# Moving one output copy, one chunk of v and one fill unit inside the step of a recurrent-memory transformer kernel

## The chip, the cores and the metric

The kernel runs on one core of one Trainium2 chip. The core has a matrix engine (TensorE, PE in the profile, with its weight loads shown apart as PEld), a vector engine (VectorE, DVE), a scalar engine (ScalarE, ACT), a general engine (GpSimd, POOL) and a queue engine (SyncE, SP) that issues most of the transfers. Each engine works through its own instructions in the order in which they were written; semaphores tie the engines together. The metric is the device time of one execution in microseconds (us), as the median of several runs.

## The reference

The input x has 2048 tokens of width 640. The first half of the computation is an attention with 32 heads of width 128 that goes through the tokens in 64 segments of 32, one after the other, and carries a memory of 8 rows from each segment to the next:

```python
for s in range(n_seg):
    xs = x[:, s * seg_len:(s + 1) * seg_len, :].copy()     # the layer-normed tokens
    h = jnp.concatenate([mem, xs], axis=1)                 # 8 memory rows and 32 tokens
    q = jnp.einsum('btd,dhe->bhte', h, Wq)
    k = jnp.einsum('btd,dhe->bhte', h, Wk)
    v = jnp.einsum('btd,dhe->bhte', h, Wv)
    scores = jnp.einsum('bhqe,bhke->bhqk', q, k) * scale
    scores = jnp.where(mask[None, None], scores, -1000000000.0)
    p = _softmax(scores, axis=-1)
    o = jnp.einsum('bhqk,bhke->bhqe', p, v)
    o = jnp.einsum('bhte,hed->btd', o, Wo)
    mem = o[:, :M, :].copy()
    outs.append(o[:, M:, :])
```

The memory rows of one segment's output are an input of the next segment, so the 64 segments are a chain. The second half adds the result to x, applies a second layer norm and a feed-forward layer (640 to 1728 and back, squared ReLU), and adds again. Everything is held in bf16, with sums in f32.

## The kernel before

The kernel has a start, 64 steps (one for each segment, function `step(b, sp)`, where segment s = 4 b + sp, so a block b of 128 tokens has the steps sp = 0 to 3), and the feed-forward part at the end. The change touches only the body of a step. There is no scheduler: the order in which the instructions are written is the order in which each engine runs them.

**What a step projects.** The 40 rows of a segment are split. 32 of them (8 memory rows and the first 24 tokens) are the "main" rows: `hT4s[b][:, c, sp, :]` holds them transposed, in five chunks c of 128 features. The last 8 tokens of each segment, the "tail" rows, don't depend on the memory. They are projected for four segments at once, ahead of time.

The projections go through `proj` (line 203): a chunk is four matmuls of 128x512 on the four column groups of TensorE. A half projection, five chunks, goes into one bank of the pool `mm`, which has three banks; ScalarE copies it out as a row (`evac_row`, lines 219 and 221; line 410 for the second half of k), and VectorE turns the row into qT or kT (`flip`, line 224; line 413). A step begins with half 0 of q, half 0 of k, half 1 of q and half 1 of k. Then come both halves of v, with the scores between their chunks. The copies of v's halves are on ScalarE, lines 508 (half 0) and 529 (half 1).

**Memory queries.** They come in two groups, n = 0 (even) and n = 1 (odd). For each group: `scores` (line 423), `soft1` (maximum on VectorE, line 429; exponential on ScalarE, line 432), `soft2` (lines 438 to 445, all on VectorE; the last one, pTm, is the transposed probabilities), `values` (lines 454 and 459 on TensorE, into the tile po) and `values_out` (n = 0 on VectorE, line 210; n = 1 on ScalarE, line 212), which puts them into oT. v's half 0 is an input of the even values.

**Token queries.** Their scores (line 499) go into the tile sk. Their softmax is lines 533 to 536 on VectorE, 551 on ScalarE, 553 and 557 on VectorE and 559 and 562 on POOL. The values of the step before are made one step late, in `token_values` (lines 359 and 364), and copied into oT by `token_out` (line 368, ScalarE): one half at the end of the step, the other at the start of the next.

**Output projection.** `wo_rounds` (line 235) runs 16 rounds of four matmuls of 128x320 into the tile pw: rounds 0 to 5, then token and odd memory values, then rounds 6 and 7, a fill unit, and rounds 8 to 15. pw holds two partial sums in its two lower and two upper groups of partitions, 32 rows each.

**From pw two things are made.** `mem_to_hT` (lines 252 to 255) makes the memory rows of the next step: VectorE transposes pw (two of line 252, tile otr), ScalarE copies the upper half (two of line 253, tile otc), VectorE adds (two of line 255) into hT. The next step's first matmul needs these. `wo_out` makes the whole output: ScalarE copies the upper half of pw to SBUF (line 242, tile otmp), VectorE adds it to the lower half (line 243, tile o, one of a ring of five), and `store_main` (line 346) issues two transfers on SP that store the 24 main token rows. otmp lives in the same buffer (tag "tk") as otr, and pw in the same bank (pool `chn`) as the next step's memory scores.

**Fill units.** The tail rows' projections (`tail_units`: v in sp = 0, q in sp = 1, k in sp = 2) and the output projection of four steps' tails (`wo_tail_units`, sp = 3) are cut into units, a chunk each or one to two wo rounds, and queued in the list `fill`. For the blocks 1 to 14 ten units are queued in the steps sp = 1 (q), 2 (k) and 3 (wo); in sp = 0 there are ten units of v in the blocks 4, 6, 8, 10 and 12, five in the blocks 5, 7, 9, 11, 13 and 14, and none in the others. `run(fill, 1)` runs one unit between rounds 7 and 8 and `run(fill, 100)` the rest at the end of the step, where they give TensorE work while the memory rows are made. The fifth unit of a half ends with that half's copy to a row on ScalarE; its flip is put into the list `late`, which the next step works off at several places.

**Other lists.** `win` holds the PE transposes of a normalised block or of tail rows: five transposes and their copies on ScalarE (line 189 for a block's rows, in the steps sp = 1; line 183, two copies, for tail rows, in two steps sp = 2). `mid` holds some normalisations. `owed` holds work of this step that the next one does: the second `token_out`, the turned token probabilities (lines 576 to 581) and `tokens_kept` (line 372).

The end of a step in the order before: `mem_to_hT`, lines 557 to 562, `wo_out` and `store_main`, `token_out` half 0, the transposes in `win` and their copies, the copies of tail q and k into qT and kT on POOL (`tails_in`, lines 328 and 330), `mid`, `fill`.

Of the kernel before, what the change touches and what calls it, by code (L numbers as in the profile page):

```python
# [16 lines left out]
def kernel(  # L17
# [25 lines left out]
    DC = D // 128  # L43
# [31 lines left out]
    wv = wts.tile([128, DC * HE], BF16)  # L75
# [117 lines left out]
    def proj(w, by, lhs, n, ps, c0, c1):  # L193

        if by == "columns":
            wr = w[:].rearrange("p (c g j n k e) -> p c n k g j e", c=DC, g=G, n=2, j=4, k=4)
        elif by == "half":
            wr = w[:].rearrange("p (c k j n e) -> p c n k j e", c=DC, k=G, n=2, j=4)
        else:
            wr = w[:].rearrange("p (c k n f) -> p c n k f", c=DC, k=G, n=2)  # L200
        for c in range(c0, c1):
            for k in range(4):
                nc.tensor.matmul(ps[32 * k:32 * k + 32, :], lhsT=lhs(c), rhs=wr[:, c, n, k], start=(c == 0), stop=(c == DC - 1))  # L203

    def mmtile():
        return mm.tile([128, 512], F32, tag="mm", name="ps")
# [31 lines left out]
    def wo_out(pw):  # L238
        o = o_ring[0]
        o_ring.append(o_ring.pop(0))  # L240
        tmp = s1.tile([128, DH], F32, tag="tk", name="otmp")
        nc.scalar.copy(out=tmp[0:64], in_=pw[64:128, 0:DH])
        nc.vector.tensor_tensor(out=o[:], in0=pw[0:64, 0:DH], in1=tmp[0:64], op=ALU.add)
        return o
# [12 lines left out]
    fill, late, mid, win, owed = [], [], [], [], [[], [], []]  # L257

    def run(q, n):
        while n > 0 and q:  # L260
            q.pop(0)()
            n -= 1
# [81 lines left out]
    def store_main(o, s):  # L344
        for ch in range(2):
            nc.sync.dma_start(out=o_all[s * SEG:s * SEG + HD, ch * DH:(ch + 1) * DH],
                              in_=o[32 * ch + M:32 * ch + 32, :])
# [37 lines left out]
    def step(b, sp, v=None):  # L385
        s = b * 4 + sp
        last = s == NS - 1
        hT4 = hT4s[b]
        lhs = lambda c: hT4[:, c, sp, :]
# [46 lines left out]
        def soft2(n):  # L436
            rm = s2.tile([128, 1], F32, tag="rm", name="rm")
            nc.vector.reciprocal(out=rm[:], in_=zms[n][:])
            pm = s2.tile([128, 2 * SEG], BF16, tag="pmem", name="pmem")
            nc.vector.tensor_scalar(out=pm[:, 0:SEG], in0=ems[n][:, 0:SEG], scalar1=rm[:, 0:1], scalar2=None, op0=ALU.mult)  # L440
            nc.vector.scalar_tensor_tensor(out=pm[:, SEG:2 * SEG].rearrange("p (j k) -> p j k", k=TL),
                                           in0=ems[n][:, SEG:NK].unsqueeze(1).to_broadcast([128, 4, TL]),
                                           scalar=rm[:, 0:1], in1=same[:], op0=ALU.mult, op1=ALU.mult)
            pT = s2.tile([128, 2 * SEG], BF16, tag="pTm", name="pTm")
            nc.vector.transpose(out=pT[:], in_=pm[:])
            return pT
# [64 lines left out]
        if not ready:  # L511
            ps1 = mmtile()
# [7 lines left out]
            run(fill, DC)  # L520
        po = pop.tile([128, G, 512], F32, tag="po", name="po")
        if not ready:
            proj(wv, "half", lhs, 1, ps1, 2, 3)
        if not last:
            values(0, pT0, po)
            values_out(0, po)
        if not ready:
            proj(wv, "half", lhs, 1, ps1, 3, DC)
            nc.scalar.copy(out=v[:, 512:1024], in_=ps1[:])  # L529
        if not last:  # L530
            pT1 = soft2(1)
        tk = s1.tile([128, HG, NK], F32, tag="tk", name="tk")
# [5 lines left out]
        pw = chn.tile([128, 512], F32, tag="ch", name="pw")  # L538
# [15 lines left out]
        if not last:  # L554
# [6 lines left out]
        pk = s1.tile([128, HG, 32], BF16, tag="pk", name="pk")  # L561
        nc.gpsimd.tensor_tensor(out=pk[:], in0=ek[:, :, 0:SEG], in1=rk[:].unsqueeze(2).to_broadcast([128, HG, SEG]),
                                op=ALU.mult)
        o = wo_out(pw)
        if s > 1:
            store_main(o, s - 2)
        if s:
            token_out(0, po)
            owed[0].append(lambda: token_out(1, po))
# [17 lines left out]
            tails_in((s + 1) // 4, (s + 1) % 4)  # L587
        run(mid, 2)
        run(fill, 100)
        if last:  # L590
            for q in owed:
                run(q, 100)
# [157 lines left out]
    for b in range(NB):  # L750
        for sp in range(4):
# [47 lines left out]
            if 2 <= e <= NK4 + 1:  # L799
                late.append(lambda e=e: prep_stats0(e - 2))  # L800
                mid.append(lambda e=e: prep_norm0(e - 2))
            step(b, sp, v0 if b + sp == 0 else None)

    def end_output(s):
# [112 lines left out]
```

## Time and profile before

| | |
|---|---|
| median of three runs | 1025.73 us (1023.66 to 1028.19) |
| the profiled execution's own time | 1020.01 us |
| its span | 1018.2 us |
| granted TensorE clock, mean | 0.998 |
| PE busy | 956.1 us (94%) |
| DVE busy | 697.4 us (68%) |
| ACT busy | 561.6 us (55%) |
| POOL busy | 261.6 us (26%) |

The profile shows one execution. A row of its groups, timeline and waits names the engine, the line of the kernel, the tile written and the tiles read, the shape of one instruction and how many there are, its busy time or duration, and in square brackets or behind the bar how long the engine stood idle before it and what it waited for. A row of the waits has the total idle time, the number of waits and the longest. A row of the windows has the length of the stretch and, for each engine, busy time and number of instructions, then the granted clock, the share of the DMA engines and GB/s. Busy time of TensorE counts overlapping matmuls once, and the ends of matmuls are modelled, so a busy TensorE may still be waiting for something. The share of the chain that ended last which falls on TensorE is 63%, on VectorE 15%, on ScalarE 12%.

### The profile page before, as it was taken

What the parts mean: (1) busy time and instruction counts of PE and PEld (TensorE: products, weight loads), DVE (VectorE), ACT (ScalarE), POOL (GpSimd) and SP (SyncE); (2) the same over time, 40 slices, a digit from 0 to 9 for tenths busy, and PEclk for the clock granted to TensorE, in tenths of its full rate; (3) what the DMA queues carried; (4) which work ended last, traced back from release to release, by engine and by line L of the source; (5) the groups of instructions that cost most, each with busy time, mean ns of one, the idle gap of its engine ahead of it and who ended that gap; (6) DMA issues with size and microseconds to landing.
All of it is one profiled execution on the core that took longest, in us unless ns stands there. A gap on an engine that the chain in (4) does not pass through costs nothing.

```text
span 1018.2 us, 55552 instructions
## 1 busy us (share of the span) xinstructions
PE 956.1 (94%) x24920; PEld 566.9 (56%) x24920; DVE 697.4 (68%) x2122; ACT 561.6 (55%) x1355; POOL 261.6 (26%) x798
## 2 busy tenths in 40 slices
PE   5789899999999999999999999999999999999998
PEld 2345466554555556555555765555755565555565
DVE  2267777776777777767777777776777788566532
ACT  3345565656665656566655566656666655533431
POOL 1012222232222222323222223222222233343210
PEclk9999999999999999999999999999999999999999
DMA  9951000000000010000000010001010110612200
GB/s 363 399 181 27 16 13 19 19 19 11 29 13 24 13 28 20 21 15 19 23 10 26 7 34 8 28 8 33 8 29 8 47 34 7 203 57 65 78 27 27
DMA packets 39199, 51.38 MB, mean 50 GB/s; under 512 B 6064, under 2 KB 35120, under 8 KB 37040
## 3 DMA queue, kind: packets, MB, share of 16 engines
q1 hardware_dynamic: 38080, 47.48, 14.1%
q8 instruction: 195, 3.19, 1.3%
q14 instruction: 44, 0.36, 0.1%
q10 hardware_dynamic: 880, 0.34, 0.1%
HBM read 38.37 MB, written 9.44 MB: 47 GB/s over the span
## 4 chain that ended last, share of the span: by engine, by line
PE 63%; DVE 15%; ACT 12%; DMA 5%; issue 3%; SPq 1%; ACTq 0%; POOL 0%; DVEq 0%; POOLq 0%
PE ps L203 25%; PE pw L235 16%; PE y L868 5%; PE ps L836 5%; PE ps L235 3%; ACT oT L368 3%; ACT row L221 3%; PE po L454 2%; DMA vt_d<-row 2%; DVE kT L413 2%; DVE kT L224 2%; PE po L359 2%; ACT otc L253 2%; DVE qT L224 2%; ACT row L219 2%
## 5 line engine op out<-in xcount | busy, mean ns | idle before, releaser
L203 PEld LDWEIGHTS <-hT 128*32 128x32 bf16 x7680 | 213.3, 96 | 169.7 <-issue 26.2
L235 PE MATMUL pw<-wo,oT 128*32 128x320 bf16 x4224 | 184.0, 301 | 7.1 <-issue 4.0
L203 PE MATMUL ps<-wv,hT 128*32 128x512 bf16 x2520 | 178.2, 379 | 1.0 <-ACT v L508 0.7
L203 PE MATMUL ps<-wq,hT 128*32 128x512 bf16 x2520 | 161.3, 381 | 15.6 <-DVE hT L255 8.4
L203 PE MATMUL ps<-wk,hT 128*32 128x512 bf16 x2520 | 160.3, 380 | 0.7 <-ACT hnT L670 0.4
L235 PEld LDWEIGHTS <-oT 128*32 128x32 bf16 x4224 | 97.8, 96 | 68.8 <-DVE oT L210 23.3
L224 DVE STREAM_TRANSPOSE qT<-row 128x512 bf16<-128x512 bf16 x128 | 89.1, 696 | 58.9 <-ACT row L219 58.1
L559 POOL TENSOR_TENSOR pkt<-ek,rk 128x64 bf16<-128x64 bf16 x64 | 19.0, 296 | 421.5 <-DVE rk L557 421.5
L219 ACT ACTIVATE row<-ps 128x512 bf16<-128x512 f32 x156 | 92.6, 605 | 48.6 <-PE ps L203 48.0
L203 PEld LDWEIGHTS <-hTt 128*32 128x32 bf16 x1920 | 54.5, 97 | 41.3 <-issue 3.1
L379 POOL COPY qz<-qT 128x96 bf16<-128x96 bf16 x126 | 33.5, 266 | 170.6 <-DVE qT L224 109.4
L368 ACT CAST oT<-po 128x512 bf16<-128x512 f32 x128 | 75.5, 590 | 1.6
L253 ACT COPY otc<-otr 64x40 f32<-64x40 f32 x126 | 28.0, 223 | 76.6 <-DVE otr L252 76.2
L221 ACT CAST row<-ps 128x512 bf16<-128x512 f32 x115 | 66.1, 595 | 3.4 <-PE ps L203 3.2
L868 PE MATMUL y<-wq,wk 128*128 128x320 bf16 x416 | 61.1, 299 | 0.4 <-DVE wk L845 0.3
L553 DVE TENSOR_REDUCE zk<-ek 128x8 f32<-128x320 bf16 x64 | 31.1, 486 | 42.2 <-ACT ek L551 42.2
L410 ACT CAST row<-ps 128x256 bf16<-128x256 f32 x126 | 40.7, 375 | 31.3 <-PE ps L203 29.3
L224 DVE STREAM_TRANSPOSE kT<-row 128x512 bf16<-128x512 bf16 x65 | 46.0, 708 | 17.1 <-ACT row L221 14.6
L432 ACT ACTIVATE em<-sm,mx 128x40 bf16<-128x40 f32 x126 | 37.1, 294 | 35.2 <-DVE mx L429 34.4
L423 PEld LDWEIGHTS <-qz 128*32 128x32 bf16 x2016 | 36.8, 95 | 32.0 <-POOL qz L379 5.0
L529 ACT CAST v<-ps 128x512 bf16<-128x512 f32 x63 | 36.9, 586 | 28.9 <-PE ps L203 28.9
L212 ACT CAST oT<-po 128x128 bf16<-128x128 f32 x63 | 16.8, 266 | 65.3 <-PE po L459 65.3
(112 smaller groups left out, 1675.5 us busy)
## 6 DMA issues: line engine op xcount, KB each, us to landing
wv<-in_A_Wv_dram SPq DMA_DIRECT2D x5, 1024.0 KB
wq<-in_A_Wq_dram SPq DMA_DIRECT2D x5, 1024.0 KB
wk<-in_A_Wk_dram SPq DMA_DIRECT2D x5, 1024.0 KB
vt<-vt_d SPq DMA_DIRECT2D x60, 64.0 KB
xt<-in_A_x_dram SPq DMA_DIRECT2D x20, 160.0 KB
vt_d<-row SPq DMA_DIRECT2D x22, 128.0 KB
wo<-in_A_Wo_dram SPq DMA_DIRECT2D x2, 1280.0 KB
wo<-in_A_Wo_dram SPq DMA_DIRECT2D x4, 640.0 KB
```

Of the source, the lines that this page charges most:

```text
L203: nc.tensor.matmul(ps[32 * k:32 * k + 32, :], lhsT=lhs(c), rhs=wr[:, c, n, k], start=(c == 0), stop=(c == DC - 1))
L219: nc.scalar.mul(out=row, in_=ps, mul=scale)
L221: nc.scalar.copy(out=row, in_=ps)
L224: nc.vector.transpose(out=dst[:, n * 16:(n + 1) * 16, 0:32], in_=row.rearrange("p (h e) -> p h e", e=32))
L235: nc.tensor.matmul(pw[32 * j:32 * j + 32, 0:DH], lhsT=lhs(p), rhs=wov2[:, head(p), ch], start=(h == 0), stop=(h == 15))
L253: nc.scalar.copy(out=tc_[:, a], in_=tr[64:128, a, :, 0:M])
L368: nc.scalar.copy(out=oTg[:, n, :, :, M:NK], in_=po[:, :, n * 128:(n + 1) * 128].rearrange("p g (j q) -> p g j q", q=32))
L410: nc.scalar.copy(out=row[:, u * 256:(u + 1) * 256], in_=ps[:, u * 256:(u + 1) * 256])
L432: nc.scalar.activation(out=em[:], in_=sms[n][:, 0:NK], func=ACT.Exp, bias=mx[:, 0:1], scale=1.0, accum_out=zm[:])
L529: nc.scalar.copy(out=v[:, 512:1024], in_=ps1[:])
L836: nc.tensor.matmul(ps[:], lhsT=w1[:, c, fc * 128:(fc + 1) * 128], rhs=hnT[:, c, :], start=(c == 0), stop=(c == DC - 1))
L868: nc.tensor.matmul(y[:, hh, 0:DH], lhsT=f1T[:, fc, k * 128:(k + 1) * 128], rhs=w2[:, fc, cs], start=(fc == 0), stop=False, skip_group_chec ...
```

## The change

Three moves inside `step`, none of which adds or removes an instruction:

- Half 1 of v has five chunks. Of these, chunks 0 and 1 are issued ahead of the odd scores, as before. Ahead of the even memory values there was chunk 2, with chunks 3 and 4 behind them; now chunks 2 and 3 stand ahead and chunk 4 behind.
- Behind chunk 4 and the copy of v's half 1, one fill unit runs if more than seven units are queued; in such a step one unit less is left for the end.
- `wo_out` and `store_main`, so the ScalarE copy of line 242, the VectorE add of line 243 and the two stores on SP, are issued at the end of the step behind `token_out`, `win`, `tails_in`, `mid` and all fill units with their row copies, where they stood directly behind lines 559 and 562.

```diff
@@ -520,13 +520,15 @@
             run(fill, DC)
         po = pop.tile([128, G, 512], F32, tag="po", name="po")
         if not ready:
-            proj(wv, "half", lhs, 1, ps1, 2, 3)
+            proj(wv, "half", lhs, 1, ps1, 2, 4)
         if not last:
             values(0, pT0, po)
             values_out(0, po)
         if not ready:
-            proj(wv, "half", lhs, 1, ps1, 3, DC)
+            proj(wv, "half", lhs, 1, ps1, 4, DC)
             nc.scalar.copy(out=v[:, 512:1024], in_=ps1[:])
+        if not last and len(fill) > 7:
+            run(fill, 1)
         if not last:
             pT1 = soft2(1)
         tk = s1.tile([128, HG, NK], F32, tag="tk", name="tk")
@@ -561,9 +563,6 @@
         pk = s1.tile([128, HG, 32], BF16, tag="pk", name="pk")
         nc.gpsimd.tensor_tensor(out=pk[:], in0=ek[:, :, 0:SEG], in1=rk[:].unsqueeze(2).to_broadcast([128, HG, SEG]),
                                 op=ALU.mult)
-        o = wo_out(pw)
-        if s > 1:
-            store_main(o, s - 2)
         if s:
             token_out(0, po)
             owed[0].append(lambda: token_out(1, po))
@@ -587,6 +586,9 @@
             tails_in((s + 1) // 4, (s + 1) % 4)
         run(mid, 2)
         run(fill, 100)
+        o = wo_out(pw)
+        if s > 1:
+            store_main(o, s - 2)
         if last:
             for q in owed:
                 run(q, 100)
```

## The prediction

> **What bounds the kernel now.** I read the page's busy table first, then the windows of one cycle of four steps, then the waits of TensorE and ScalarE, then the timeline around the joints between steps.
>
> ```profile
> PE 956.1 (94%) x24920; PEld 566.9 (56%) x24920; DVE 697.4 (68%) x2122; ACT 561.6 (55%) x1355; POOL 261.6 (26%) x798
> ```
>
> TensorE (PE) carries the kernel, but 94% hides the idle time that can be won: a matmul's row lasts 0.38 us although the next one starts 0.054 us later. So I ask for the length of each kind of step.
>
> ```profile
> 271.70:285.03 13.33, 13.02 (x379) 7.16 (x371) 9.53 (x30) 8.87 (x23) 4.27 (x15) 1.00 0.16 46
> 285.03:297.56 12.53, 12.41 (x368) 7.32 (x371) 9.41 (x30) 7.51 (x20) 2.17 (x10) 1.00 0.07 19
> 297.56:310.19 12.63, 12.51 (x398) 7.66 (x393) 9.88 (x31) 7.98 (x21) 3.28 (x13) 1.00 0.02 5
> 310.19:321.93 11.74, 11.43 (x356) 6.23 (x345) 9.48 (x32) 6.82 (x18) 3.60 (x12) 1.00 0.05 12
> ```
>
> Each row runs from the first q matmul of a step to that of the next: sp = 1, 2, 3 and 0. The steps sp = 1 and 2 issue the same projections and fill units, sp = 1 five transposes more (0.38 us from the first to the fill behind them), and yet it is 0.80 us longer. The waits of TensorE, then of ScalarE (us in total, times, longest):
>
> ```profile
> PE ps L203 <- DVE hT L255: 8.4, 12, 1.2
> PE ps L203 <- ACT hT L189: 4.5, 14, 0.6
> ```
>
> ```profile
> ACT otmp L242 <- DVE hT L255: 19.5, 62, 0.3
> ```
>
> Fourteen q projections wait for a ScalarE copy (L189), and ScalarE itself stands still 0.31 us in each of 62 steps in front of the whole output's copy (otmp, L242). The joint at the end of an sp = 1 step:
>
> ```profile
> 282.33 0.58 DVE L252 STREAM_TRANSPOSE otr<-pw 128x160 f32<-128x160 f32 x2
> 282.59 2.13 PE L203 MATMUL ps<-wq,hTt 128*32 128x512 bf16 x36
> 282.71 0.45 ACT L253 COPY otc<-otr 64x40 f32<-64x40 f32 x2 [0.99 <-DVE otr L252]
> 283.48 0.42 ACT L242 COPY otmp<-pw 64x320 f32<-64x320 f32 x1 [0.32 <-DVE hT L255]
> 283.93 0.59 ACT L368 CAST oT<-po 128x512 bf16<-128x512 f32 x1
> 283.94 0.48 DVE L243 TENSOR_TENSOR o<-pw,otmp 64x320 bf16<-64x320 f32 x1 [0.31 <-ACT otmp L242]
> 284.41 0.56 ACT L189 COPY hT<-pt 128x480 bf16<-128x480 bf16 x1
> 284.86 1.11 ACT L219 ACTIVATE row<-ps 128x512 bf16<-128x512 f32 x2
> 285.03 1.26 PE L203 MATMUL ps<-wq,hT 128*32 128x512 bf16 x20 [0.31 <-ACT hT L189]
> ```
>
> ScalarE goes otc, (idle) otmp, L368, L189, and only then may q start. Two more places: the joint behind an sp = 2 step, and the even memory values (L454) behind a chunk of v.
>
> ```profile
> 298.55 0.71 DVE L224 STREAM_TRANSPOSE kTt<-row 128x512 bf16<-128x512 bf16 x1 [0.62 <-ACT row L221]
> 299.61 0.71 DVE L224 STREAM_TRANSPOSE qT<-row 128x512 bf16<-128x512 bf16 x1 [0.35 <-ACT row L219]
> 300.57 0.71 DVE L224 STREAM_TRANSPOSE kT<-row 128x512 bf16<-128x512 bf16 x1
> ...
> 407.69 0.41 PE L203 MATMUL ps<-wv,hT 128*32 128x512 bf16 x4
> 407.93 0.25 DVE L445 STREAM_TRANSPOSE pTm<-pmem 128x64 bf16<-128x64 bf16 x1
> 408.22 0.26 PE L454 MATMUL po<-pTm,v 32*128 32x8 bf16 x16
> ...
> 420.31 0.41 PE L203 MATMUL ps<-wv,hT 128*32 128x512 bf16 x4
> 420.66 0.26 PE L454 MATMUL po<-pTm,v 32*128 32x8 bf16 x16
> ```
>
> Here VectorE has 0.62 and 0.35 us of slack before its flips. The chunk streams for 4 x 0.054 = 0.22 us, so TensorE stands idle 0.53 - 0.22 = 0.31 us before the values at 408.22 (VectorE's pTm ends at 408.18) and 0.35 - 0.22 = 0.13 us at 420.66.
>
> **The change part by part.** t is the start of the first otr transpose; all times are us.
>
> *Whole output's copy behind the fill copies, sp = 1 joint (14 of these).* Before: otc ends t+0.83, hT is added by 1.06, otmp runs from 1.15, L368 from 1.60, L189 from 2.08 to 2.64, q from 2.70. After: L368 needs nothing of otmp and follows otc at 0.85, L189 at 0.85 + 0.48 = 1.33 (the spacing of the rows), ends at 1.89, so q may start at 1.95. TensorE: the fill starts at 0.26; 36 matmuls end streaming at 0.26 + 36 x 0.054 = 2.20, the 32 that are left at 1.99. So q starts at about 2.00, 0.70 earlier: 14 x 0.70 = -9.8. From the row's idle time alone (0.31) and the unit moved out (0.22) it would be 0.53, or -7.4; from ScalarE's path alone 0.75, or -10.5. I take the starts, which rest on no modelled end.
>
> The row's 0.31 is counted from the end of the last fill matmul. The Trainium skill, Perfetto Trace Analysis, section "Tensor Engine Instruction (MATMUL, LD_WEIGHTS)", says that this end is computed from the instruction's size and not observed; by the row the whole sum below would be -9.1, by the starts -11.5, and starts 0.054 apart under rows of 0.38 agree with the page.
>
> *The same at the two joints with tail transposes* (q waits 1.31 for ACT hTt L183 at 455.29): L183 loses otmp and its wait in front, 0.73 each: -1.5. The fill there ends long before.
>
> *ScalarE behind it.* otmp now stands in front of the next q row (L219). In the sp = 1 joint the fill rows start at 1.33 + 0.45 = 1.78 and about 2.36 (the last fill matmul starts at 1.93 and its row lasts 0.38), otmp runs from 2.85 to 3.27; the q row is due at 2.00 + 1.31 = 3.31. Hidden, with 0.04 to spare. In the sp = 2 joint otmp runs 2.37 to 2.79 and q's row is due at 2.81.
>
> *VectorE behind it.* The add (L243, 0.48) waits for otmp, and the flips queue behind it: add from 3.31, fill flip from 3.72, qT from 4.34, which is 2.34 after q; before it was 287.04 - 285.03 = 2.01. Behind the sp = 2 joint: add 2.83, fill flip 3.24, qT 3.86, 2.36 after q (before 2.05). The next flip, kT, began 3.00 after q because its row came then; now pTt (0.14 to kT) ends in front of it at about 3.13. So the chain of flips that ends in pTm, and with it the values, is 0.13 later in the 28 steps sp = 2 and 3: +3.6. Ends: 0, when the slack takes all of it, and 0.48, the whole add: 0 to +13.4. I take 0.13 since both joints give it. In sp = 0 and 1 VectorE queues at most one normalisation there, and the values wait for TensorE.
>
> *The chunk of v ahead of the values.* The second chunk (0.22) fills the 0.13 of idle time in the other steps, so the values come 0.09 later: 31 x 0.09 = +2.8 (28 with VectorE late, and the three sp = 1 steps in which a normalisation delays pTm, are left out). Behind VectorE's 0.31 it costs nothing. From the values to otr nothing gets shorter: wo starts 0.71 after the values, for L210's evacuation; TensorE has values, one chunk and a fill unit, 0.67, under it, as it had two chunks before. In the 14 steps with seven fill units or fewer no unit comes, and the same wait of 0.71 has less work under it; that is their +0.09.
>
> *The fill unit moved.* One unit less stands behind the last wo matmuls. sp = 2 (12 steps that aren't tail joints) and the five sp = 0 steps with ten units are bound there by TensorE: 17 x -0.22 = -3.7. In sp = 3 the units are wo rounds of 4 or 8 matmuls at 0.034 (60 of them from 412.02 to the q at 414.06): the eight (0.27) go into the later gap, which had 0.08 idle behind four, +0.06, and the end loses 0.27: 14 x -0.21 = -2.9. The unit's bank was copied out (L508) before the values.
>
> *Other queues.* The two stores of the output on SP now follow the v fill's stores, and the loads of x and vt behind them move with them by up to 1.7 (the add ends at 3.79, not at 2.09); x is used two steps later at the earliest, vt in the next block. POOL's copies (L328, L330) wait for nothing moved. The next even scores (same bank as pw) start 4.3 after q; the add ends 1.8 after it.
>
> Sum: -9.8 - 1.5 + 3.6 + 2.8 - 3.7 - 2.9 = -11.5. The profiled execution took 1020.01 (span 1018.2), so 1008.5 on its scale; it lies 5.7 under the median of the runs, 1025.73, and the difference carried to that gives 1014.2. With both ends: -10.5 - 1.5 + 0 + 2.8 - 6.6 = -15.8 (1009.9) and -7.4 - 1.5 + 13.4 + 2.8 - 6.6 = +0.7 (1026.4).
>
> **The rivals.**
> *The add takes it back.* If all 0.48 of L243 stays in line in front of the flips, the 28 steps cost 13.4, not 3.6: -1.7, 1024.0. For it: VectorE's flips run back to back from kT to pTm. Against: 0.62 and 0.35 idle ahead of them.
> *The joint isn't freed.* L368 or L189 starts no earlier, since another wait ends last there: -11.5 + 11.3 = -0.2, 1025.5. Against: ScalarE idles 0.3 for hT alone, which only otmp needs (its buffer is otr's).
> *Slower.* The margin of 0.04 at q's row breaks: otmp (0.42) delays the row and the add (0.48) the flip, 0.90 in line in all 28 steps, 28 x 0.77 = +21.6 on my sum: +10.1, 1035.8. It decides once the flips are over 0.72 late (28 x 0.59 = 16.6). For it: fill rows that end late push otmp. Against: q's row moves with q, and VectorE's idle time.
> *More.* The slack swallows the 0.13: -15.1, 1010.6.
>
> **How the numbers follow.** Forecast as summed 0.60, more 0.10, add takes it back 0.13, joint not freed 0.07, slower 0.10. Half a per cent is 5.1 us, about what a measurement of this kernel can tell from no change (its runs spread over 4.5). Faster 0.70, same 0.20, slower 0.10. Predicted 1014.2. Range: from the low end less the runs' reach under their median (2.1) to the two middle rivals: 1007.5 to 1026.5, which leaves out the slower case and the edges.
>
> **What would show it.** Right: the sp = 1 windows shrink from 13.3 to about 12.7, the sp = 2 and 3 windows by 0.1, small sp = 0 windows grow by 0.1; the wait of otmp for hT is gone; q no longer idles for L189. Wrong: L454 waits for pTm by more than 0.3, L219 of q starts later than 1.4 after q, or L243's idle time grows while kT starts over 3.3 after q.

## The result, and the profile after

The changed kernel takes 1011.27 us (median of four runs, 1011.22 to 1012.38), beside 1024.69 for the kernel before in the same comparison: a ratio of 0.9868, with a 95% interval of 0.9838 to 0.9899, or 13.4 us less. In a later comparison, with more runs, the two medians are 1011.34 and 1022.26 (ratio 0.9905, 0.9882 to 0.9927; 10.9 less). The forecast was 11.5 less, 1014.2.

The profiled execution took 1011.23 us, with a span of 1009.4. This is 8.8 under the span of before; the profile of before lay 4.7 under the median 1024.69, and the section on the reasons says what is known of that. The busy table hardly moves:

```profile
PE 956.7 (95%) x24920; PEld 568.9 (56%) x24920; DVE 687.1 (68%) x2122; ACT 559.3 (55%) x1355; POOL 258.3 (26%) x798
```

The windows of the same four steps, from the first q matmul of a step to that of the next (sp = 1, 2, 3, 0; length, then PE, PEld, DVE, ACT, POOL, clock, DMA share, GB/s):

```profile
268.65:281.60 12.95, 12.95 (x380) 9.53 (x375) 8.99 (x29) 8.56 (x22) 3.71 (x13) 1.00 0.16 47
281.60:293.98 12.38, 12.38 (x373) 6.85 (x368) 9.45 (x30) 7.93 (x21) 2.68 (x11) 1.00 0.08 20
293.98:306.47 12.49, 12.49 (x397) 7.38 (x392) 9.46 (x30) 8.00 (x21) 3.27 (x12) 1.00 0.02 5
306.47:318.54 12.07, 11.67 (x359) 8.52 (x347) 9.69 (x32) 6.88 (x19) 3.78 (x13) 1.00 0.04 11
```

They were 13.33, 12.53, 12.63 and 11.74. The sp = 1 step gives 0.38, the next two 0.15 and 0.14, and the sp = 0 step, which has few fill units, is 0.33 longer. In this sp = 1 and this sp = 0 step the even values come 0.11 later than in the quietest of their kinds (6.92 after q, not 6.81). Those, from 475.03 and from 614.42, are 12.84 and 11.96 long, where the same steps took 13.32 and 11.74 before. The waits of TensorE, then of VectorE (us in total, times, longest):

```profile
PE ps L203 <- DVE hT L255: 8.4, 12, 1.2
PE pw L235 <- DVE o L243: 1.7, 1, 1.7
```

```profile
DVE o L243 <- ACT otmp L242: 87.5, 66, 3.8
DVE qT L224 <- ACT row L219: 20.8, 22, 12.6
```

Before, the last two were:

```profile
DVE o L243 <- ACT otmp L242: 25.5, 66, 2.5
DVE qT L224 <- ACT row L219: 58.1, 59, 13.5
```

The wait of q for L189 (4.5 before) is gone, and of otmp's wait for hT (19.5) 0.3 is left. One wait is new: 1.7 us of a wo matmul for L243, once. VectorE now waits in front of the add, and its wait for q's row has shrunk. Most of the slack in front of the flips has been used up. The sp = 1 joint in the timeline:

```profile
279.60 0.58 DVE L252 STREAM_TRANSPOSE otr<-pw 128x160 f32<-128x160 f32 x2
279.87 1.91 PE L203 MATMUL ps<-wq,hTt 128*32 128x512 bf16 x32
279.99 0.45 ACT L253 COPY otc<-otr 64x40 f32<-64x40 f32 x2 [0.99 <-DVE otr L252]
280.34 0.57 ACT L368 CAST oT<-po 128x512 bf16<-128x512 f32 x1
280.82 0.55 ACT L189 COPY hT<-pt 128x480 bf16<-128x480 bf16 x1
281.60 1.25 PE L203 MATMUL ps<-wq,hT 128*32 128x512 bf16 x20
282.51 0.42 ACT L242 COPY otmp<-pw 64x320 f32<-64x320 f32 x1
282.95 0.60 ACT L219 ACTIVATE row<-ps 128x512 bf16<-128x512 f32 x1
282.96 0.48 DVE L243 TENSOR_TENSOR o<-pw,otmp 64x320 bf16<-64x320 f32 x1 [2.06 <-ACT otmp L242]
283.37 0.69 DVE L224 STREAM_TRANSPOSE qTt<-row 128x512 bf16<-128x512 bf16 x1
284.00 0.66 DVE L224 STREAM_TRANSPOSE qT<-row 128x512 bf16<-128x512 bf16 x1
```

From otr to q it is 281.60 - 279.60 = 2.00; it was 2.70. ScalarE goes otc, L368, L189 without a stop. otmp ends at 282.93, and q's row starts at 282.95: the margin forecast at 0.04 is 0.02. The add, the fill flip and qT follow back to back. The even values of the next step, whose q is that at 281.60:

```profile
287.89 0.62 PE L203 MATMUL ps<-wv,hT 128*32 128x512 bf16 x8
288.15 0.25 DVE L445 STREAM_TRANSPOSE pTm<-pmem 128x64 bf16<-128x64 bf16 x1
288.45 0.26 PE L454 MATMUL po<-pTm,v 32*128 32x8 bf16 x16
```

Two chunks stream for 0.43, and the values start 0.56 after the first of them, 6.85 after q; VectorE's pTm ends at 288.40, 6.80 after q. The two engines now arrive together. At the end of step 63, which has no next step, stands the new wait:

```profile
868.94 0.44 PE L235 MATMUL pw<-wo,oT 128*32 128x320 bf16 x5 [1.22 <-issue]
869.32 0.45 PE L671 MATMUL pt<-ident,hn 128*128 128x128 bf16 x5
869.81 0.69 ACT L672 COPY hnT<-pt 128x640 bf16<-128x640 bf16 x1 [2.35 <-PE pt L671]
870.52 0.42 ACT L242 COPY otmp<-pw 64x320 f32<-64x320 f32 x1
870.98 0.48 DVE L243 TENSOR_TENSOR o<-pw,otmp 64x320 bf16<-64x320 f32 x1 [3.50 <-ACT otmp L242]
871.51 3.75 PE L235 MATMUL pw<-wo,oT 128*32 128x320 bf16 x64 [1.74 <-DVE o L243]
875.19 0.37 PE L359 MATMUL po<-pTk,v 32*128 32x32 bf16 x32
```

Here pw has to be read out before the next 64 wo matmuls may write its bank, and otmp is queued behind the copy of line 672. The same place in the profile of before:

```profile
880.07 0.45 PE L669 MATMUL pt<-ident,hn 128*128 128x128 bf16 x5
881.31 2.36 PE L235 MATMUL pw<-wo,oT 128*32 128x320 bf16 x64 [0.79 <-DVE pTt L576]
883.60 0.37 PE L359 MATMUL po<-pTk,v 32*128 32x32 bf16 x32
```

From the transposes (L671; L669 before) to L359 it is 5.87, where the profile of before has 3.53. And the 64 matmuls take 3.75, where before they took 2.36. The windows of the 64 matmuls, after and then before, show why (the third column from the end is the granted clock):

```profile
871.51:875.19 3.68, 3.68 (x64) 2.43 (x64) 0.42 (x2) 0.04 (x1) 0.78 (x3) 0.61 1.05 380
```

```profile
881.31:883.60 2.29, 2.29 (x64) 1.53 (x65) 0.33 (x2) 1.04 (x2) 0.84 (x3) 1.00 1.01 324
```

Summed over the steps of the two profiles (each from its first q to that of the next):

| steps | change, us | by the forecast's terms |
|---|---|---|
| 14 of sp = 1 | -7.5 | -8.6 |
| 11 of sp = 2 and 2 tail joints | -3.6 | -2.3 |
| 13 of sp = 3 | -1.4 | -1.1 |
| 13 of sp = 0 | +0.8 | +0.3 |
| the first four and the last five, and the start | +0.8 | |
| from the q of step 63 to the end | +2.1 | 0 |
| sum | -8.8 | |

The third column groups the terms of the forecast over all of their steps, so for one or two steps more than the second (for sp = 1: -9.8 for the joints and 13 x 0.09 for the chunk).

### The profile page after: what moved, and what is told of

Read it like the earlier page. It is cut to its first block, busy times and chain, and to the rows that moved or that the text cites. A ratio compares the mean times of both kernels' runs of the same rounds, so it can differ in the third digit from the quotient of the medians.

```text
span 1009.4 us, 55618 instructions
## 1 busy us (share of the span) xinstructions
PE 956.7 (95%) x24920; PEld 568.9 (56%) x24920; DVE 687.1 (68%) x2122; ACT 559.3 (55%) x1355; POOL 258.3 (26%) x798
## 4 chain that ended last, share of the span: by engine, by line
PE 83%; DMA 5%; DVE 5%; ACT 4%; issue 2%; SPq 1%; POOL 0%; ACTq 0%; DVEq 0%; POOLq 0%
PE ps L203 42%; PE pw L235 16%; PE y L870 5%; PE ps L838 5%; PE ps L235 4%; DMA vt_d<-row 2%; PE po L454 2%; PE po L359 2%; PE sm L423 2%; PE ps L499 1%; DMA wo<-in_A_Wo_dram 1%; DMA om<-in_A_mem_dram 1%; ACT row L219 1%; ACT otc L253 1%; DVE otr L252 1%
## 5 line engine op out<-in xcount | busy, mean ns | idle before, releaser
L203 PEld LDWEIGHTS <-hT 128*32 128x32 bf16 x7680 | 219.9, 96 | 153.2 <-DVE hT L255 13.6
L235 PE MATMUL pw<-wo,oT 128*32 128x320 bf16 x4224 | 184.7, 303 | 9.4 <-issue 4.1
L235 PEld LDWEIGHTS <-oT 128*32 128x32 bf16 x4224 | 99.6, 97 | 69.2 <-DVE oT L210 23.7
L561 POOL TENSOR_TENSOR pkt<-ek,rk 128x64 bf16<-128x64 bf16 x64 | 19.2, 300 | 426.8 <-ACT oT L368 396.7
L243 DVE TENSOR_TENSOR o<-pw,otmp 64x320 bf16<-64x320 f32 x66 | 31.8, 481 | 86.4 <-ACT otmp L242 86.4
L368 ACT CAST oT<-po 128x512 bf16<-128x512 f32 x128 | 73.7, 577 | 0.2 <-PE pw L235 0.2
L224 DVE STREAM_TRANSPOSE kT<-row 128x512 bf16<-128x512 bf16 x65 | 44.8, 690 | 12.3 <-ACT row L221 11.2
## 6 DMA issues: line engine op xcount, KB each, us to landing
wv<-in_A_Wv_dram SPq DMA_DIRECT2D x5, 1024.0 KB
wq<-in_A_Wq_dram SPq DMA_DIRECT2D x5, 1024.0 KB
wk<-in_A_Wk_dram SPq DMA_DIRECT2D x5, 1024.0 KB
```

Of the source, the lines that this page charges most:

```text
L224: nc.vector.transpose(out=dst[:, n * 16:(n + 1) * 16, 0:32], in_=row.rearrange("p (h e) -> p h e", e=32))
L235: nc.tensor.matmul(pw[32 * j:32 * j + 32, 0:DH], lhsT=lhs(p), rhs=wov2[:, head(p), ch], start=(h == 0), stop=(h == 15))
L368: nc.scalar.copy(out=oTg[:, n, :, :, M:NK], in_=po[:, :, n * 128:(n + 1) * 128].rearrange("p g (j q) -> p g j q", q=32))
```

## The experiments

**The output's move alone.** The chunk and the fill unit stay as before.

```diff
-        o = wo_out(pw)
-        if s > 1:
-            store_main(o, s - 2)
...
         run(fill, 100)
+        o = wo_out(pw)
+        if s > 1:
+            store_main(o, s - 2)
```

> Of the three moves only the whole output's: chunk of v and fill unit as before. Theory (the joint is freed): in the sp = 1 joint q starts when the 36 fill matmuls have streamed, 2.20 to 2.25 after the first otr transpose, and not at 2.70: 14 x -0.47 = -6.6 us; the two joints with tail transposes -0.85 each, -1.7; the values of the steps sp = 2 and 3 come up to 0.07 later, +2.0 at most; the last step's output now holds the bank of the closing projection, +2.3. Sum -4.0: about 1020.5 us with before at 1024.7. Rival (the add takes it back: the flips are 0.48 late in 28 steps): +9.4 us, 1034. Rival (the gain of the whole change lies in the fill unit and the chunk): 1024 to 1027.

Measured: 1016.28 (1012.19 to 1020.25) against 1022.03, ratio 0.9938 (0.9905 to 0.9971). In the trace the quiet sp = 1 step (one without extra work, here from 267.59) is 12.95 long. All 36 fill matmuls still stand in front of q there (2.20 of streaming instead of 1.99), and q starts 1.15 after hT, where it was 1.63: 0.48 earlier, not 0.70. The sp = 2 and 3 steps hardly move (12.59 and 12.62, against 12.53 and 12.63). So the joint is freed by this part, and the last 0.2 needs the fill unit to leave. The time is 5.8 less, where 4.0 was expected, which the interval takes in; the six runs spread over 8 us, so its size says no more than that.

**The chunk alone.**

```diff
-            proj(wv, "half", lhs, 1, ps1, 2, 3)
+            proj(wv, "half", lhs, 1, ps1, 2, 4)
...
-            proj(wv, "half", lhs, 1, ps1, 3, DC)
+            proj(wv, "half", lhs, 1, ps1, 4, DC)
```

> Only the chunk of v. What the prediction said: it fills 0.13 us of idle time, so the values of the 31 steps that TensorE bounds come 0.09 later: +2.8 us, 1027.5, with the values at 6.69 after q in a quiet sp = 1 step (before 6.60). Theory from the trace after: the 0.13 is no idle time but the price of going from one tile shape to the next, it is paid all the same, and the whole chunk of 0.22 delays the values (6.82): 34 x 0.22 = +7.5 and in the steps sp = 2 and 3 +0.06 x 28 = +1.7: about 1034 us. Rival: what the chunk costs ahead it gives back behind: 1024.7.

Measured: 1024.76 (1022.4 to 1026.44) against 1022.03, ratio 1.0019 (1.0001 to 1.0037): 2.7 slower. In the timeline of the sp = 1 step that starts at 273.07:

```profile
279.32 0.63 PE L203 MATMUL ps<-wv,hT 128*32 128x512 bf16 x8
279.32 0.25 DVE L445 STREAM_TRANSPOSE pTm<-pmem 128x64 bf16<-128x64 bf16 x1
279.88 0.26 PE L454 MATMUL po<-pTm,v 32*128 32x8 bf16 x16
```

VectorE's pTm is done at 279.57, well ahead, and the values still come 0.56 after the first of the eight matmuls; behind four it was 0.35. The 0.13 between the end of the streaming and the values is there with four and with eight. It was not idle time that a chunk could fill. The chunk so costs its whole 0.22 in such a step: the quiet sp = 1 step is 13.54 long, the sp = 0 step 11.96. In sp = 2 and 3 the values come at 6.82, 0.03 later. The step is thus as expected here, but the time is not: 31 steps at 0.22 are 6.8 and some 9 was expected in all, where 2.7 was measured (0.1 to 3.8), which is the +2.8 of the prediction. In the waits of TensorE the stops put down to "issue" fell from 10.6 to 7.9 in all, which is two thirds of the missing 4.1; whether the chunk caused that was not tested.

**The fill unit alone.**

```diff
+        if not last and len(fill) > 7:
+            run(fill, 1)
```

> Only the fill unit, behind two chunks of v. The output projection starts when TensorE has run values, two chunks and the unit, 0.93 after the values and not 0.71: +0.22 in each of the 48 steps with more than seven units. It comes back at the end of sp = 2 and sp = 0, where TensorE bounds the joint, and in sp = 3 all but 0.05; in the 14 sp = 1 joints and the two with tail transposes ScalarE bounds q, and it is lost: 16 x 0.22 + about 0 = +3.5 us: 1028. Rival (the unit runs in idle time before the output projection and is won there): 48 x -0.2, 1015.

Measured: 1025.57 (1021.9 to 1027.28) against 1022.03, ratio 1.0028 (1.0009 to 1.0047): 3.5 slower. The unit puts off the first wo matmul (7.49 instead of 7.31 after q in a quiet sp = 1 step), and in sp = 1 nothing is given back: q still waits for ScalarE, 1.63 after hT, and the wait for L189 grows from 4.5 to

```profile
PE ps L203 <- ACT hT L189: 7.8, 15, 0.8
```

In sp = 2, where TensorE sets the joint, the step is 12.48 against 12.53. So this part pays only where TensorE is what q waits for, and it is the output's move that makes TensorE so in sp = 1. The chunk alone puts the first wo matmul at 7.53, and so do both together in the changed kernel: the two delays are not added. So there the unit behind the chunk costs nothing more, and what it takes from the end of the step is won. The three parts alone come to -5.8 + 2.7 + 3.5 = +0.4; together they gave -13.4 and -10.9.

**The output ahead of the fill rows.** The changed kernel, with the output's copy behind the transposes' copies but in front of the tails, the fill units and their rows.

```diff
         for f in outs:
             f()
+        o = wo_out(pw)
+        if s > 1:
+            store_main(o, s - 2)
...
         run(fill, 100)
-        o = wo_out(pw)
-        if s > 1:
-            store_main(o, s - 2)
```

> The changed kernel, with the whole output behind token_out and the copies of the transposes, but ahead of the fill units' copies. Theory (what counts is that L368 and L189 go ahead of otmp; the place against the fill rows does not matter): q starts 2.00 after the first otr transpose in sp = 1 as in the changed kernel, the values of sp = 2 and 3 are bound by TensorE at 6.85 and 6.82 and stay there: 1011.3 within 1.5 us; the wait of the add (line 243) for otmp, 87.5 us in the changed kernel, falls to under 50. Rival (the fill rows must go first, for their banks or for q's row): 1013 to 1017. Rival (VectorE's lateness is the limit in sp = 2 and 3, so the earlier add wins): 1008 to 1010.

Measured: 1011.71 (1009.05 to 1012.38) against 1022.03, ratio 0.9886 (0.9851 to 0.9922), the same as the change. q stands 0.94 after hT in sp = 1, as in the changed kernel. VectorE's wait in front of the add falls to 50.3 us (under 50 was expected) and its wait for q's row is 36.6, so the slack of the flips is back in part; the values of sp = 2 come 6.81 after q, 0.04 earlier. The gain thus lies in clearing ScalarE in front of L189; whether the add comes in front of the fill's rows or behind them is worth almost nothing.

**The change once more, in a later comparison.**

> The changed kernel once more, beside the others of this call: 1011.3 us within 1.5.

Measured: the 1011.34 against 1022.26 given above. Its profile again has a quiet sp = 1 step of 12.85, sp = 2 of 12.38.

**The add twice.** L243 is issued twice in every step, the second time with the same result.

```diff
-        nc.vector.tensor_tensor(out=o[:], in0=pw[0:64, 0:DH], in1=tmp[0:64], op=ALU.add)
+        for _ in range(times):
+            nc.vector.tensor_tensor(out=o[:], in0=pw[0:64, 0:DH], in1=tmp[0:64], op=ALU.add)
...
-        o = wo_out(pw)
+        o = wo_out(pw, 2)
```

> The changed kernel with the add of line 243 issued twice, so VectorE has 0.41 us more in front of the flips in every step; nothing else changes. Theory (TensorE bounds the values of sp = 2 and 3 at 6.85 and 6.82, and VectorE has under 0.06 to spare there): the values of these 28 steps come 0.35 to 0.41 later, +10 to +11.5 us: about 1022. The rival that decided the prediction's slower case would show the same price. Rival (VectorE has the 0.6 and 0.35 of slack that the timeline of the kernel before shows): no change, 1011.3.

Measured: 1031.46 (1029.55 to 1032.26) against 1022.26, ratio 1.0094 (1.0073 to 1.0114): 20.1 slower than the changed kernel of the same comparison, twice what was expected. VectorE in the sp = 2 step whose q starts at 286.29 (the lines of this kernel are one higher):

```profile
287.65 1.00 DVE L244 TENSOR_TENSOR o<-pw,otmp 64x320 bf16<-64x320 f32 x2 [2.06 <-ACT otmp L242]
288.57 0.69 DVE L224 STREAM_TRANSPOSE qTt<-row 128x512 bf16<-128x512 bf16 x1
...
293.36 0.24 DVE L446 STREAM_TRANSPOSE pTm<-pmem 128x64 bf16<-128x64 bf16 x1
```

The second add takes 0.92 - 0.41 = 0.51 from its place in the queue to the fill flip, and not the 0.41 that I had priced. pTm ends 293.60 - 286.29 = 7.31 after q, 0.51 later than in the changed kernel. Nothing of it is absorbed: the quiet sp = 2 and 3 steps are 12.89 and 12.95 long, 0.51 and 0.52 more, and sp = 0 and 1 do not move (12.34 and 12.84). Against the profile of the changed kernel on the same chip, the 26 steps sp = 2 and 3 from the sixth to the 56th take 13.8 more, sp = 0 and 1 together 3.9, the five steps after them 2.4, and the end 1.2. The 13.8 are near 26 x 0.51 = 13.3; the rest is not explained. VectorE has no slack left in sp = 2 and 3: that the add did not take the gain back was not due to a large reserve.

**The last step as before.** The changed kernel, with the output's copy in step 63 in its old place.

```diff
+        if last:
+            store_main(wo_out(pw), s - 2)
         if s:
             token_out(0, po)
...
-        o = wo_out(pw)
-        if s > 1:
-            store_main(o, s - 2)
+        if not last:
+            o = wo_out(pw)
+            if s > 1:
+                store_main(o, s - 2)
```

> The changed kernel, with the whole output of the last step alone back in its old place. Theory (there the closing projection takes the bank of pw at once, so it waits for the add, 1.7 us, and its half of the token values stands behind otmp): the stretch from the transposes ahead of the closing projection to the last token values shrinks from 5.9 to about 3.5 us, the kernel by 2.3: 1009. Rival (the loads of the feed-forward weights end the stretch anyway): 1011.3.

Measured: 1009.36 (1004.85 to 1011.29) against 1022.26, ratio 0.9874 (0.9852 to 0.9896), 2.0 below the changed kernel of the same comparison. That is the size expected, but the intervals overlap, and the profile does not bear out the reason. The wait of 1.74 is 0.79 again, as before, and yet the 64 matmuls take 4.03 us at a granted clock of 0.57:

```profile
867.11 0.45 PE L235 MATMUL pw<-wo,oT 128*32 128x320 bf16 x5 [2.01 <-issue]
867.49 0.45 PE L674 MATMUL pt<-ident,hn 128*128 128x128 bf16 x5
868.74 4.03 PE L235 MATMUL pw<-wo,oT 128*32 128x320 bf16 x64 [0.79 <-DVE pTt L577]
```

In this execution the stop in front, put down to "issue", was 2.01 instead of 1.22. So my reading that the move had cost 2.3 in the last step mixed a wait (0.95) with a fall of the clock (1.4) that the old order can have too.

**Everything that pays.** The last step as before, the output in front of the fill rows, and the second chunk ahead of the values only where more than seven fill units are queued.

```diff
+        ahead = 4 if len(fill) > 7 else 3
...
-            proj(wv, "half", lhs, 1, ps1, 2, 4)
+            proj(wv, "half", lhs, 1, ps1, 2, ahead)
...
```

> Three edits on the changed kernel: chunk 3 of v goes ahead of the even values only in the steps that have a fill unit to put behind them; the whole output stands behind the transposes' copies but ahead of the fill rows; in the last step it stands where it was. Theory: 14 steps lose the 0.22 of the chunk, -3.1, less what TensorE's own issue waits take back; the last step -2.3; the place ahead of the fill rows 0 to -1: about 1006.5 us. Rival (the chunk ahead costs nothing, as the run with it alone, +0.2%, may be read): 1009.

Measured: 1008.62 (1006.61 to 1010.04) against 1022.26, ratio 0.9871 (0.9851 to 0.9892). The sp = 0 steps with few units are back at 11.74. The median lies 2.7 below the changed kernel's, nearer to the rival's 1009 than to the 1006.5 expected, and can't be told from that of the kernel with only the last step as before. In this profile too the clock fell in the last step.

**Work in the last step's gap.** The kernel with the last step as before, and four matmuls into a bank that nobody reads, where TensorE waits 0.79 us.

```diff
+        if last:
+            warm = mmtile()
+            for i in range(4):
+                nc.tensor.matmul(warm[:], lhsT=ident[:], rhs=wo[:, 0, 0:512], start=(i == 0), stop=(i == 3))
```

> The last step as before (the output's copy directly behind lines 559 and 562 in step 63 alone) and, in that step, four matmuls 128x512 of the identity with a chunk of wo into a bank of their own behind the five transposes of hn; their result is used by nothing. They put work into the 0.79 us in which TensorE waits for pTt. Theory: in the last step the granted clock falls to 0.50 for some 3.4 us because TensorE stands still twice in a row (1.22 to 2.01 for no visible reason, then 0.79), and the 64 matmuls of wo behind it take 3.75 to 4.03 us instead of 2.36. With the second stretch filled the clock stays at 1.00 and the 64 matmuls take about 2.4: 1.4 less than the kernel with the last step as before, so about -14 against before, and no dip of the clock between the last wo rounds and line 359. Rival: the first stretch alone, or the transfers of the feed-forward weights, bring the clock down; then the dip stays, the 64 matmuls take 3.7 to 4.0, and the time is that of the kernel with the last step as before, about -12.9 against before.

Measured: 1007.19 (1005.84 to 1010.6) against 1024.41, ratio 0.9839 (0.9813 to 0.9866): 17.2 less, where 14 were expected, which the interval takes in. It is the lowest median of all, though its interval overlaps with those of the two kernels before it. In the profile the clock holds, and the 64 matmuls are at 2.36 again:

```profile
866.46 0.45 PE L235 MATMUL pw<-wo,oT 128*32 128x320 bf16 x5 [1.28 <-issue]
866.83 0.45 PE L678 MATMUL pt<-ident,hn 128*128 128x128 bf16 x5
867.12 1.03 PE L590 MATMUL ps<-wo,ident 128*128 128x512 bf16 x4
868.08 2.36 PE L235 MATMUL pw<-wo,oT 128*32 128x320 bf16 x64
```

```profile
868.08:870.37 2.29, 2.29 (x66) 1.53 (x66) 0.33 (x2) 1.03 (x2) 0.83 (x3) 1.00 1.00 331
```

By itself this would not decide it, since the stop in front is 1.28 here, and with 1.22 and 0.79 the profile of before kept its clock without any such work. The next run does.

**The same in the changed kernel,** with eight matmuls in the wait of 1.74.

> The changed kernel with eight such matmuls (1.73 us) behind the transposes of hn in the last step, where TensorE waits 1.74 us for the whole output's add. It parts the price of the change in the last step (from the transposes of hn to line 359 5.87 us where the profile of before had 3.53) into the longer wait and the clock. Theory: the clock stays at 1.00, the 64 matmuls take 2.36 instead of 3.75, line 359 comes 4.4 to 4.5 us after the transposes; the time is 1.4 below the changed kernel, about -12.3 against before. Rival: the clock falls all the same: line 359 at 5.9 behind the transposes, about -10.9 against before.

Measured: 1011.07 (1007.73 to 1013.92) against 1024.41, ratio 0.9874 (0.9848 to 0.99); 13.3 less than before, where -12.3 was expected, and -10.9 by the rival. Its profile:

```profile
867.39 1.89 PE L588 MATMUL ps<-wo,ident 128*128 128x512 bf16 x8
869.30 2.36 PE L235 MATMUL pw<-wo,oT 128*32 128x320 bf16 x64
871.59 0.37 PE L359 MATMUL po<-pTk,v 32*128 32x32 bf16 x32
```

The stop in front was 1.51, more than the 1.22 of the changed kernel, and the clock stayed at 1.00. From the transposes to L359 it is 4.48: the wait of 0.95 is still paid, the 1.4 of the clock is not. That settles what the 5.87 was made of, in the executions that were profiled. This one is one of two of the six whose mean granted clock was 1.000 (1007.73 and 1007.74 us); the other four, at 0.995 and 0.996, took 1010.65 to 1013.92, and where their clock fell is not on record. The transfers fill the DMA engines beside the 64 matmuls as they do in the changed kernel (share 1.06 and 1.05), so they don't bring the clock down by themselves. In time the gain can't be told from the run-to-run spread of this kernel.

## Why the prediction was right

**The sp = 1 joint: right, to the hundredth.** It was to be 2.00 from otr to q, and it is 2.00. The starts decided, as chosen; the row's idle time would have given 0.53, and so 2.17 from otr to q. The Trainium skill, Perfetto Trace Analysis, "Tensor Engine Instruction (MATMUL, LD_WEIGHTS)", says that the profiler estimates a matmul's end; that the starts gave 0.70 and the row's end 0.53 agrees with it. ScalarE ran as laid out (L368 0.74 behind otr, where 0.85 was forecast, otmp 2.91 against 2.85, q's row 3.35 against 3.31).

**The tail joints:** 0.85 each (q after hT from 2.64 to 1.79) instead of 0.73.

**VectorE: the direction right, the size too large.** In sp = 2 qT comes 2.40 after q (forecast 2.34, before 2.01) and kT 3.12, as forecast (3.13), but pTm ends at 6.80, where it was at 6.75, and the values come 0.06 later, not 0.13: what I took for a queue without a gap from kT to pTm gave back 0.07. In sp = 3 kT starts at 3.05 and pTm ends at 6.74, as before. The values there are 0.03 later, but that is the chunk: with the chunk alone they also come at 6.82, with the output's move alone at 6.79, as before. So VectorE costs 14 x 0.06 = 0.8 instead of 3.6. With that its queue is full in both, as the doubled add shows.

**The chunk: the term that was wrong.** "The second chunk (0.22) fills the 0.13 of idle time" was wrong. The 0.13 is not idle time but a part of the way from a projection to the values, and it comes behind eight matmuls as behind four. The term is 31 x 0.22 = 6.8, not 2.8, and 14 x 0.03 = 0.4 in sp = 3, before the other stops of TensorE move. With it the sp = 1 steps should give 6.9 and not 8.6; they gave 7.5. The changed kernel without the chunk at all was not run.

**The fill unit: right.** sp = 2 gave 0.15 with its values 0.06 later, so the unit gave 0.21 (forecast 0.22); sp = 3 gave 0.14 to 0.17 with its values 0.03 later, so 0.17 to 0.20 (forecast 0.21).

**Missing: the last step.** The sum moved the output in all joints, without asking who reads behind it in step 63, where pw is wanted at once. In the two profiles that is +2.3: 0.95 of waiting and 1.4 of clock.

**How these add up.** With the measured sizes the sum is -9.8 - 1.7 + 0.8 + 7.2 - 3.7 - 2.9 + 2.3 = -7.8, against the -8.8 of the two profiles; "issue" stops are 1.0 less after than before. The medians differ by more, 10.9 and 13.4. One part of that is probably the clock: the last step of the profiled execution of before kept it, but in the profiles of the chunk alone, the fill unit alone and the last step as before it fell there, with the same order in that step. So other executions of before probably pay the 1.4 too, and the difference of these two profiles is too small by about that: 8.8 + 1.4 = 10.2, near the 10.9. What is left to the 13.4 is not explained; its interval is 10.3 to 16.6. Errors of both signs thus met near the forecast: the total is more exact than its terms.

**The rivals.** The add took back 0.8, not 13.4. The joint was freed: L368 follows otc at once. The slower case did not come, but it was close: 0.02 of margin at q's row, and no slack on VectorE (0.51 more per step costs 0.51). "More" has the right sign of its reason, since the slack swallowed half of the 0.13 in sp = 2 and all of it in sp = 3, but the chunk's price took that back.

**The signs and the range.** Of the signs of being wrong, L243's idle time did grow (25.5 to 87.5), but kT starts 3.29 after q at the latest (steps 5 to 57), just under the 3.3 that was to go with it; q's row starts 1.35 after q in the joint shown, 0.05 under its bound. The low end less 2.1 is 1007.8, not 1007.5, and the upper edge of 1026.5 lies above both middle rivals (1024.0 and 1025.5), beside the high end of the sum.

## What to carry to other kernels

Take a copy that nobody waits for out of the queue of the engine that the next step's first matmul waits for, and look who reads behind it in the last iteration as well. A part that puts work elsewhere is worth its time only where that engine then sets the end: here the fill unit lost alone and paid with the other two, and the chunk made room for it, but cost its full price in the steps without a unit. A short gap in front of an instruction is free to fill only if it shrinks when something is put into it; the same gap behind two different lengths of work is a price, not slack.

## What the runs showed of the hardware

- **The granted clock is set in fixed windows, and short stops in one window add up.** In the clock records of the twelve traces, up to 1000 us, every fall lasts 3.41 us (one twice that), and the stretches at full clock between two falls are whole multiples of it. The last step of the changed kernel and then of the kernel before, cut on each trace's own grid:

```profile
867.57:870.99 3.42, 0.97 (x17) 0.48 (x11) 0.01 (x1) 1.14 (x3) 0.87 (x2) 1.00 1.01 278
870.99:874.40 3.41, 2.89 (x45) 1.97 (x48) 0.94 (x3) 0.56 (x1) 0.78 (x3) 0.50 1.04 366
```

```profile
876.60:880.01 3.41, 2.19 (x87) 1.34 (x80) 1.00 (x3) 0.47 (x1) 0.87 (x2) 1.00 1.07 389
880.01:883.43 3.42, 2.63 (x71) 1.81 (x69) 0.96 (x3) 2.09 (x4) 0.84 (x3) 1.00 0.93 253
```

In the changed kernel TensorE was busy for 0.28 of one window (0.97 of 3.42, by the rows and their modelled ends), since the stop of 1.22 and the first 1.22 of the stop of 1.74 lie in it, and the clock fell. Before, the boundary at 880.01 lay between the stops of 1.22 and 0.79: 0.64 and 0.77, and no fall. Cut in this way, each of the 28 windows of these traces with a busy share of 0.40 or less is followed by a fall to 0.50, and none of the other 3419, at 0.42 or more, is. The last step as before had 0.35 (2.01 and 0.79 in one window); with the second stop filled it was 0.62 and 0.68. The grid begins 15.7 to 19.2 us into the trace, elsewhere in each execution, so the same two stops can cost a fall in one and none in the next. The Trainium skill, TensorE: Matmul & The Clock Gate, "What's actually happening", has a clock that is halved after an idle window of about 3.4 us. The half and the length agree; but none of the 28 windows was wholly idle (0.19 to 0.40 busy), and no stop in a last step was longer than 2.35 us. The mean granted clock of a run, which such dips lower, goes with its time: of the 21 runs of before beside the first four experiments, the nine at 0.993 to 0.995 average 1023.6 us and the twelve at 0.996 to 1.000 average 1021.1.
- **A projection costs the values behind it 0.13 us more than its streaming,** whether it has four or eight matmuls (0.35 and 0.56 from its first matmul to the values, at 0.054 each). The shape of the tiles changes there, from 128*32 to 32*128; whether that is the cause was not tried.
- **TensorE stops for 0.2 to 2.1 us where the profile shows no releaser** ("issue"), some 8 to 12 us in all in each of the twelve profiles, mostly at the small matmuls of L235 and L454. Counted through all of TensorE's recorded instructions in the order of their starts, weight loads too, the instruction that starts late is the 194th to 196th of a block of 256 in 230 of the 234 stops. The profile's DMA queue named "instruction" moved 195 packets in this time, and the 49,913 instructions recorded in the changed kernel are 195 blocks of 256. This points to the supply of instructions; no run tested it, and most blocks pass without a stop. As a change moves instructions, it moves what stands at these places: the stops differ from kernel to kernel by some 4 us and can hide or double a change of this size. The chunk alone should have lost 6.8 by its quiet steps and lost 2.7.
